# Fused packed attention and gated MLP on one core: small score and weight products gathered into fewer groups on the TensorE

## The chip, the cores and the metric

The kernel runs on one core of a Trainium2 chip. A core has a TensorE (PE) for matrix products, VectorE (DVE), ScalarE (ACT) and GpSimd (POOL) for the rest, and SyncE (SP), which here only issues DMAs. Each engine works through its own list of instructions in order. Products land in PSUM, eight banks of 512 fp32 columns on 128 partitions; all else lives in SBUF. The metric is the device time of one execution in microseconds.

## The reference

There are B = 8 batches, 8 heads, 576 tokens and 64 channels a head; `p` has 32 packing rows a head. Two attentions in a row are followed by a gated MLP over all 4608 tokens.

```python
p_packed = sm_attn(p, k, v)          # 32 rows attend to 576 tokens
out = sm_attn(q, p_packed, p_packed) # 576 tokens attend to the 32 rows
x = out.transpose(0, 2, 1, 3).reshape(B * S, H * D)
h = x @ w_in                         # 512 -> 2048
g = h * np.clip(h + 3.0, 0.0, 6.0) / 6.0
return g @ w_out                     # 2048 -> 512
```

## The kernel before

**Blocks.** One batch is a block. Since the second attention's result is a product of its weights `a` and the packed values, the kernel multiplies the packed values (`pps`) with `w_in` first; that small product is called M, and a block's first big product is M times `a`. Both are kept as a high and a low fp32r part (`m_hi`, `m_lo`, `a_hi`, `a_lo`), so each product takes three matmuls.

**The first phase** is block 0 with everything that the start needs: weights are loaded and put into parts, block 0's attention and MLP are computed, and block 1's attention is prepared. Its order is written out by hand in the text `PLAN`: each word takes one step of a chain, and within it the instructions of PE, DVE, ACT, POOL and SP are issued as the words stand. `ENGINES` says which engine does some of the copies and subtractions.

**Blocks 1 to 7** run as two chunks of tokens (256 and 320 columns). The order in each engine's list is chosen by a planner when the program is built, from dependencies, priorities and what is written as fixed. In a chunk the loop goes over 16 slices f of 128 hidden columns. `first_product` (L996) writes h = M[f] a into one of two PSUM banks (`ps_hh`), at most 320 of its 512 columns; `gate_into` makes the gate from it (ACT at L1007, then DVE at L1008); the gate's parts are split on ACT, DVE and POOL; a second product (L1036) adds to four accumulator banks. Twelve slices go as six pairs in a scheme with seven products for two slices (`pair_product`, 21 matmuls of 256 columns); its combined blocks of `w_out` are T1, T2, T3 and T4, of which some are kept in DRAM and fetched again (`fetch_t`, the `wt` steps). The last four slices are single (`single_product`, 6 matmuls of 512 columns). Second products are held back in `pend` by one or two slices.

**The next block's work** is woven into this loop by `fill`, called twice for each slice. `STEPS` gives, for each block and chain, the half-slices (0 to 63 over both chunks) at which the chain takes a step:

- `in`, `pack`: loads of the next block's k, q, v, p; the first scores `u_s1`, the exponentials, the transposes `u_ets`, the product with v `u_pvs`, and `u_ppt`, which writes `pps`.
- `ahead`: the second scores `u_s2` and the softmax on DVE and ACT that makes `a`.
- `soon`, `late`: M for the next block, a quarter (4 slices, 512 columns) at a time, with `w_in` fetched again from DRAM into one buffer (`w_in0`, L1451); three quarters in this block, the fourth early in the next.

All scores and M are products of tiles with 64 rows and 32 columns of PE, eight at a time over four pairs of heads and two halves (`each_head`, matmuls at L412). In blocks 2 to 7 they are written to a PSUM pair of their own (`att_pair`), as eight separate groups per block: two halves of 288 columns of the first scores, two of the second, and four quarters of M. In each group the PE order is fixed (`manual_schedule`).

**Room.** The next block's loads of k, q and v go through two SBUF buffers with the tag `nat`. M has four homes of a quarter each, which change roles between even and odd blocks (`m_tiles`).

Of the kernel before, what the change touches and what calls it, by code (L numbers as in the profile page):

```python
# [36 lines left out]
    },  # L37
# [7 lines left out]
    },  # L45
# [7 lines left out]
    },  # L53
# [7 lines left out]
    },  # L61
# [7 lines left out]
    },  # L69
# [7 lines left out]
    },  # L77
    7: {
        "in": "",
        "pack": "",  # L80
        "ahead": "",
        "soon": "",
        "late": "2 4 6 8",
        "wt": "10 14 42 46",
# [10 lines left out]
s0 s0 warm q1 e0 q1 c0 c0 q0 e0 v0 q0 e1 v0 v0 c1 li0 a0 a0 in s1 s1 b2 qr in a0 a0 v0 z0 c1 qr z0 z0a z0a z0a  # L95
z0a e1 v1 li2 a2 a2 a2 z0a z0a v1 z0a z0a in q2 in li1 q2 q3 q3 v1 v1 z1 m0 z0a a2 z1 a1 a1 a1 z0a z0a a1 z1b
m0 z1b z1a li3 a3 a3 z1a upper m0 m0 z1b z1b a3 z1a z1b z1a m0 lo0 z0a b0 li4 a4 a4 z1a z1a a3 z1b b0 b0 z1b
z1a z1a m1 b0 lo1 b1 m2 z1b z1b z1b z1a z1a z1a li7 a7 lp z1b b1 b1 b1 h0 warm h0 a7 a7 r0 warm r0 m1 li5 m1
h1 m1 m1 y0 b0 b0 b1 r0 lo3 b3 lo5 r0 a7 h1 b3 b3 b1 x0 x0 x0 x0 r1 r1 li6 m2 m2 h2 m2 m2 h2 r1 r1 x1 x1 x1 y0
a6 a6 a6 a5 b5 a4 b3 y1 y1 a4 r2 lk0 lk2 tk0 a6 x1 r2 h3 h3 lo4 lo6 a5 a5 a5 r2 r2 x2 tk2 m4 b3 b3 x2 x2 x2  # L100
lk3 lk1 b4 b4 b4 b4 b5 b5 li8 tp r3 y3 r3 tk3 b6 m4 m4 m4 m4 h4 h4 y2 b6 r3 r3 x3 b4 b4 b5 b5 y3 r4 y4 b6 b6
x3 tk1 r4 y4 a8 a8 a8 a8 x3 below r4 S S li9 y2 x3 b5 S S S S h5 b6 b6 r4 a9 a9 a9 li10 a10 a10 a10 h5 lq1 a10
r5 r5 lo8 tq1 S x4 S a9 r5 r5 x4 x4 x4 h6 h6 b8 b8 b8 y5 r6 r6 b8 li11 a11 a11 a11 x5 x5 x5 b8 x5 a11 h7 h7
lo7 b7 r6 r6 b7 y5 r7 y7 S m8 S lo9 b9 b9 b8 b7 lq3 lo10 r7 x6 x6 x6 x6 li12 tq3 li13 m8 lq2 m8 h8 lq0 r7 m8
m8 h8 b7 b7 r7 b7 x7 x7 x7 b10 b10 y6 y6 b10 y7 lo12 lv r8 r8 r8 r8 b9 b10 a13 a13 S S b10 tq2 h9 h9 r9 r9 x8
x8 b9 a13 b10 x7 a12 x8 a12 tq0 y8 b9 r9 x8 S S S E b12 y9 y9 E b12 h10 h10 y8 r10 y10 E E E a13 r9 b9 x9 S x9
a12 a12 r10 b12 h11 E h11 r10 r10 x10 lo11 b11 b11 b11 b11 S E lw0 lw1 V r11 r11 li14 V V x10 a14 a14 a14 T T
x9 x9 Z b12 b12 li15 a15 a15 a15 x10 x10 r11 a14 Z Z Z b11 Z y11 r11 a15 lo15 b15 b15 m12 m12 b11 b15 b15 x11
x11 m12 m12 m12 h12 h12 b12 Z lo13 b13 b13 y10 b13 y11 r12 y12 r12 r12 Z b13 b13 b13 Z x11 r12 Z x11 h13 h13
x12 x12 lo14 x12 r13 r13 h14 h14 b15 b15 r13 r13 Z Z Z y12 b14 b14 b14 r14 Z Z r14 y13 x13 x13 x12 Z h15 h15  # L110
b14 Z b14 b14 x13 x13 r14 r14 x14 x14 x14 y13 r15 r15 r15 y14 Z Z r15 x15 x15 x14 Z Z Z Z o0 o1 o0 o1 y15 Z Z
Z y14 M stage M M M M y15 x15 x15 o3 o3 o2 o2
# [21 lines left out]
def packed_attention_moe(  # L134
# [38 lines left out]
    mp = [ctx.enter_context(tc.tile_pool(name="mp", bufs=1))]  # L173
# [112 lines left out]
    def coarse(part):  # L286

        for stop in part:
            if stop is None:
                yield  # L290
# [11 lines left out]
    state, steady = {}, []  # L302

    def on(name, engine):
# [7 lines left out]
    def m_tiles(b, n):  # L312
        if ("m", b, n) not in state:
            if b % 2 == 0 and n < NCH - 1:
                n_ = NCH - 2 - n
            else:
                n_ = n
# [1225 lines left out]
```

## Time and profile before

| what | value |
|---|---|
| median of three runs | 709.0 us (707.68 to 710.12) |
| the profiled execution | 707.82 us |
| its span, first to last instruction | 705.9 us |
| DVE, ACT, POOL busy | 501.0, 429.2, 383.2 us |
| DMA traffic | 107.50 MB, 152 GB/s on average |

The span is shorter than the time of the same execution by what lies before the first and after the last instruction, 1.9 us. Busy times of different engines run beside each other. A row of the view of groups gives line, engine, operation and tiles, then the count, the busy time in us, the mean length of one in ns, and the idle time of the engine before them with what ended it. In the timeline a row gives start and length in us. A matmul's length there includes its passage through the array, so that successive ones overlap: what one costs is the distance between starts.

### The profile page before, as it was taken

To read this page: it belongs to the slowest core of one execution; us is meant where nothing else is said; L and a number is where in the kernel's file an instruction comes from. 1 tells how busy PE (TensorE), PEld (TensorE's weight loads), DVE (VectorE), ACT (ScalarE), POOL (GpSimd) and SP (SyncE) were. 2 spreads that over 40 slices of the span, in tenths; PEclk is the share of its full clock that TensorE was granted. 3 is DMA by queue.
4 is the path that set the end of the run, shared out by engine and by line. 5 is a ranking of instruction groups with operands and counts; after the bars stand their busy time and mean duration, and the time that the engine had idled before them with its cause. 6 is when DMAs were issued, how large, how long until landed. Compare 5 with 4: busy or idle time off the path is not lost.

```text
span 705.9 us, 16233 instructions
## 1 busy us (share of the span) xinstructions
PE 691.9 (98%) x5944; PEld 595.6 (84%) x5944; DVE 501.0 (71%) x1093; ACT 429.2 (61%) x1013; POOL 383.2 (54%) x615
## 2 busy tenths in 40 slices
PE   8799999999999999999999999999999999999997
PEld 6587876878878988899898998899898998889997
DVE  4898778868899669765687657876488766874443
ACT  4798876546666646565466655666366664755453
POOL 2456642744645456466464554666454546657563
PEclk9999999999999999999999999999999999999999
DMA  9979952964428665554545756383443945341030
GB/s 275 333 185 269 201 141 113 281 129 116 122 105 233 139 152 206 138 154 100 122 188 149 155 127 197 121 203 86 127 166 122 183 103 182 120 137 43 32 105 31
DMA packets 199104, 107.50 MB, mean 152 GB/s; under 512 B 173424, under 2 KB 185200, under 8 KB 195440
## 3 DMA queue, kind: packets, MB, share of 16 engines
q1 hardware_dynamic: 198480, 106.26, 55.1%
q8 instruction: 47, 0.77, 0.5%
q14 instruction: 33, 0.27, 0.1%
q10 hardware_dynamic: 544, 0.20, 0.1%
HBM read 89.65 MB, written 16.78 MB: 151 GB/s over the span
## 4 chain that ended last, share of the span: by engine, by line
PE 80%; DMA 6%; DVE 6%; ACT 3%; issue 2%; POOL 2%; SPq 1%; DVEq 0%; POOLq 0%; ACTq 0%
PE acc L1036 45%; PE ps_hh L996 23%; PE ps L412 6%; PE ps_h L669 3%; DMA raw_in<-in_moe_w_in_dram 2%; PE ps L1036 2%; DMA raw_out<-in_moe_w_out_dram 1%; DMA w_again<-w_kept 1%; PE ps L532 1%; DMA nat<-in_q_dram 1%; SPq L356 1%; DMA p_nat<-in_p_dram 1%; PE ps L502 0%; ACT t L1332 0%; DVE t L1008 0%
## 5 line engine op out<-in xcount | busy, mean ns | idle before, releaser
L996 PE MATMUL ps_hh<-a_hi,m_hi 128*128 128x320 f32 (+1 forms) x448 | 133.8, 299 | 0.3 <-DVE t L1008 0.3
L996 PE MATMUL ps_hh<-a_hi,m_lo 128*128 128x320 f32 (+1 forms) x448 | 132.9, 297 | 0.0
L996 PE MATMUL ps_hh<-a_lo,m_hi 128*128 128x320 f32 (+1 forms) x448 | 132.9, 297 | 0.0
L1008 DVE SCALAR_TENSOR_TENSOR t<-t,ps_hh 128x320 f32<-128x320 f32 (+1 forms) x148 | 66.1, 447 | 75.9 <-ACT t L1007 72.3
L1036 PE MATMUL acc<-wo_hi,g 128*128 128x512 f32 x288 | 103.4, 402 | 0.0
L1007 ACT ACTIVATE t<-ps_hh,three 128x320 f32<-128x320 f32 (+1 forms) x148 | 73.7, 501 | 47.5 <-PE ps_hh L996 40.0
L1014 POOL TENSOR_TENSOR gf<-tb,gf 128x256 fp32r<-128x256 f32 x76 | 61.6, 811 | 66.6 <-ACT gf L1013 60.0
L996 PEld LDWEIGHTS ps_hh<-a_hi,m_hi 128*128 128x128 f32 x448 | 84.7, 189 | 7.6 <-DVE t L1008 2.6
L996 PEld LDWEIGHTS ps_hh<-a_lo,m_hi 128*128 128x128 f32 x448 | 84.7, 189 | 4.3 <-issue 1.4
L996 PEld LDWEIGHTS ps_hh<-a_hi,m_lo 128*128 128x128 f32 x448 | 84.7, 189 | 2.9 <-issue 2.5
L1014 POOL TENSOR_TENSOR g<-t,g 128x256 fp32r<-128x256 f32 x72 | 54.4, 758 | 37.1 <-ACT g L1013 33.8
L1036 PE MATMUL acc<-wt,ga 128*128 128x256 f32 x456 | 74.3, 283 | 0.0
L1036 PE MATMUL acc<-wo_hi,ge 128*128 128x256 f32 x304 | 71.3, 284 | 0.0
L1036 PEld LDWEIGHTS acc<-wo_hi,g 128*128 128x128 f32 x288 | 52.7, 189 | 15.4 <-POOL bnd L1032 2.5
L1036 PEld LDWEIGHTS acc<-wt,ga 128*128 128x128 f32 x456 | 63.3, 190 | 0.7 <-issue 0.5
L1014 POOL TENSOR_TENSOR ga<-t,ga 128x256 fp32r<-128x256 f32 x76 | 61.8, 814 | 1.4 <-ACT ga L1013 1.1
L1036 PEld LDWEIGHTS acc<-wo_hi,ge 128*128 128x128 f32 x304 | 53.2, 190 | 6.1 <-ACT ga L1013 2.5
L1036 PE MATMUL acc<-wo_lo,g 128*128 128x512 f32 x144 | 56.8, 395 | 0.0
L617 DVE STREAM_TRANSPOSE tr<-nat 128x576 f32<-128x576 f32 x56 | 42.6, 766 | 17.7 <-DMA nat<-in_q_dram 9.1
L1007 ACT ACTIVATE tb<-ps_hh,three 128x256 f32<-128x256 f32 (+1 forms) x76 | 38.0, 499 | 26.9 <-PE ps_hh L996 26.1
L1032 POOL COPY bnd<-t 128x64 f32<-128x64 f32 x76 | 21.8, 286 | 58.4 <-DVE t L1008 53.0
L1278 POOL TENSOR_TENSOR tb<-tb,t 128x128 f32<-128x128 f32 x76 | 38.0, 500 | 28.3 <-DVE t L1273 22.9
(226 smaller groups left out, 1844.9 us busy)
## 6 DMA issues: line engine op xcount, KB each, us to landing
w_again<-w_kept SPq DMA_DIRECT2D x24, 1024.0 KB, 4.9
wt<-t_kept SPq DMA_DIRECT2D x24, 768.0 KB, 5.0
out_dram<-osb SPq DMA_DIRECT2D x33, 256.0 KB, 2.6
nat<-in_k_dram SPq DMA_DIRECT2D x112, 72.0 KB, 2.8
nat<-in_q_dram SPq DMA_DIRECT2D x112, 72.0 KB, 2.9
raw_in<-in_moe_w_in_dram SPq DMA_DIRECT2D x10, 512.0 KB, 6.3
raw_out<-in_moe_w_out_dram SPq DMA_DIRECT2D x10, 512.0 KB, 4.9
w_kept<-w_in_sb SPq DMA_DIRECT2D x4, 1024.0 KB, 7.6
```

The lines of the kernel that those rows point to most:

```text
L356: nc.sync.dma_start(out=t[r:r + 32], in_=src[b, 2 * a + h, :, 32 * c:32 * c + 32].rearrange("(t i) j -> i t j", i=32),)
L412: nc.tensor.matmul(pair[x][NPK * a:NPK * a + NPK, :n], rows[half, a], c, start=True, stop=True)
L532: nc.tensor.matmul(pair[x][cols, :D], l, r, start=(c == 0), stop=(c == NST - 1))
L617: nc.vector.transpose(out=t, in_=state.pop(("nat", which, b, a)))
L669: nc.tensor.matmul(h[:, hf, :HS], mm[:, g, fs], aa[:, hf * HS:(hf + 1) * HS], start=(g == 0 and i == 0), stop=(g == NG - 1 and i == 2),)
L996: state["first"] = nc.tensor.matmul(h[:, :n], mm[:, g, fs], aa[:, t0:t0 + n], start=(g == 0 and i == 0), stop=(g == NG - 1 and i == 2),)
L1007: state["relu"] = nc.scalar.activation(out=t[:, :n], in_=h, func=AF.Relu, bias=three)
L1008: state["gate"] = nc.vector.scalar_tensor_tensor(out=t[:, :n], in0=t[:, :n], scalar=6.0, in1=h, op0=ALU.min, op1=ALU.mult)
L1014: engine.tensor_sub(out=lo, in0=x, in1=hi.bitcast(F32))
L1032: nc.gpsimd.tensor_copy(out=bnd[:, f, side * REM:side * REM + REM], in_=t[:, boff:boff + REM])
L1036: nc.tensor.matmul(out, lhs[x], rhs[y], start=first and i == 0, stop=last and i == 2, skip_group_check=True)
L1278: nc.gpsimd.tensor_sub(out=s4, in0=b1, in1=s2)
```

## The change

**One stay for all scores.** In blocks 2 to 7 the 576 columns of a score product are written in one fixed group. 512 go to the PSUM pair as before; 64 go beside the first products, to columns 320 to 383 of the two `ps_hh` banks that were used last (`tops`). The copies out of PSUM follow the new split.

```diff
-    def both_halves(at_once, lhs, rhs):
-
-        if at_once:
+    def all_scores(lhs, rhs, one=None):
+
+        def tokens(cols):
+            return lambda a, half: rhs[a][half].rearrange("p t i -> p (t i)")[:, cols]
+
+        pair, few, more = att_pair(), slice(NB, S), slice(0, NB)
+        beyond = [tops[x][:, SPARE:NB - P] for x in range(2)]
+        at_once(
+            lhs,
+            (beyond, tokens(few)),
+            *([([tops[x][:, NB - P:] for x in range(2)], lambda a, half: one[half, a])] if one else []),
+            (pair, tokens(more)),
+        )
+        return (few, beyond), (more, pair)
+
+    def at_once(rows, *rounds):
+
+        with tc.manual_schedule(engines={mybir.EngineType.PE}), tc.high_priority():
+            for banks, cols in rounds:
+                for a in range(NPAIR - 1, -1, -1):
+                    for x in (1, 0):
...
```

**M in three stays and a piece.** M's 16 slices are made as 1 + 5 + 5 + 5: slice 0 with the second scores (128 columns in `ps_hh`), then slices 8 to 11 with 6, 2 to 5 with 7, and 12 to 15 with 1, each stay with 512 columns in the pair and 128 in `ps_hh`. The kept `w_in` has a new layout in DRAM, and each fetch comes as a large piece (1 MB) and one slice (256 KB), the slice in a `nat` buffer. M lives in one tile for slices 12 to 15 and one for the other twelve, with a new table of homes (`m_home`, `m_at`).

```diff
+    def u_m_wide(b, f, side):
+
+        four, one = state.pop(("w4", f)), state.pop(("w1", side))
+        yield tops
+        pair = att_pair()
+        beyond = [tops[x][:, SPARE:SPARE + P] for x in range(2)]
+        at_once(
+            pps[b % 2],
+            (beyond, lambda a, half: one[half, a]),
+            (pair, lambda a, half: four[half, :, a]),
+        )
...
+    def fetch_one(f):
+        t = state["w1", f] = ap.tile([P, NPAIR, P], F32, name="w_one", tag="nat", bufs=2)
+        nc.sync.dma_start(out=t, in_=w_kept[:, f])
...
+    def soon_wide(b):
+
+        fetch_one(0)
+        yield
+        for f, side in ((8, 6), (2, 7)):
+            fetch(f, side)
+            yield
+            yield
+            yield from coarse(u_m_wide(b, f, side))
+        fetch(12, 1)
```

**Where a stay goes.** A chain that needs `ps_hh` stops before its stay and is held; the next `beside` call with room (every odd slice of a pair, every single slice) lets it go on, with its matmuls queued behind the first product just written. The gate gets high priority.

```diff
+    def go(chain):
+
+        if not any(chain is c for c in held) and next(chain, None) is tops:
+            held.append(chain)
+
+    def beside(fill, s, room=True):
+
+        if room:
+            with tc.issue_after(state["first"].ins):
+                for chain in held:
+                    next(chain)
+            held.clear()
+        fill(s + 0.5)
...
+        tops[:] = tops[-1:] + [h]
         return h[:, :n]
...
-        state["relu"] = nc.scalar.activation(out=t[:, :n], in_=h, func=AF.Relu, bias=three)
...
+        with tc.high_priority():
+            state["relu"] = nc.scalar.activation(out=t[:, :n], in_=h, func=AF.Relu, bias=three)
...
-        with tc.manual_schedule(engines={mybir.EngineType.PE}), tc.high_priority():
+        with tc.issue_after(state["turned"].ins), tc.manual_schedule(engines={mybir.EngineType.PE}), tc.high_priority():
```

The last of these stands in `u_pvs`; `turned` is the DVE copy that ends `u_ets`.

**New step tables and another order of the first phase.** All tables of `STEPS` are new (block 7 uses block 5's), and what is left of the chains is run at slice 31 instead of 31.5. `PLAN` holds the same words in another order; `ENGINES` is unchanged. The beginning of each, and one table:

```diff
-in k0 in in p p k0 k1 k1 k2 k2 lo2 in kr b2 b2 b2 b2 kr k3 k3 in in in b2 s0 s0 s0 s0 s0 s0 s1 s1 s1 s1 s1 s1
...
+in k0 in in in p lo2 k2 k0 k1 b2 in k1 in kr p kr b2 b2 k3 s0 in s0 k3 in k2 b2 s1 s0 s0 b2 s1 s1 warm s0 s1 e0
...
-        "soon": "42 44 46 48 50 52 54 56 58 60 62 62",
-        "late": "2 4 6 8",
-        "wt": "10 14 42 46",
...
+        "soon": "31 39 39 44 47 53 53 53 54 55 55 55",
+        "late": "1 6 7 13 15 15 20",
+        "wt": "14 23 45 47",
...
```

More of the change, by code (lines that the diff above doesn't have):

```diff
@@ L99 @@
[L99 to L103, printed above, removed]
@@ L113 @@
+x14 r15 x14 r15 Z Z x14 r15 x15 Z x15 x14 Z Z Z Z o0 o1 Z M Z o0 y14 o1 y13 stage M M y15 M x15 M x15 y15 o2 o3
+o2 o3
 """
 ENGINES = {
[9 rows of a table removed]
[10 rows of a table added]
 }
@@ L310, in copy, with more_m, m_home, m_at @@
         (engine.copy if engine is nc.scalar else engine.tensor_copy)(out=dst, in_=src)
[L312 to L317, printed above, removed]
-            j = (n_ + 1) % NCH if b else 0
-            state["m", b, n] = tuple(
-                mp[j > 0].tile([P, NG, NB], F32R, name=f"m_{part}", tag=f"m_{part}{j}") for part in ("hi", "lo")
-            )
-        return state["m", b, n]
+    m_room = []
+    def more_m(pool, n):
+        m_room.append({
+            part: pool.tile([P, NG, n * NB], F32R, name=f"m_{part}", tag=f"m_{part}{len(m_room)}") for part in ("hi", "lo")
+        })
+    more_m(mp, 1)
+    def m_home(b, f):
+        if b == 0 or f >= 3 * FPC:
+            return 0, f % FPC
+        if b == 1:
+            return 1, (f + 2 * FPC) % (3 * FPC)
+        if f < 2:
+            return 1, 11 - f
+        near = (8, 9, 10, 11, 6)
+        if f in near:
+            return 1, near.index(f) + FPC * (b % 2) + b % 2
+        return 1, (2, 3, 4, 5, 7).index(f) + 5 * (1 - b % 2)
+    def m_at(part, b, f, n=1):
+        room, at = m_home(b, f)
+        return m_room[room][part][:, :, at * P:(at + n) * P]
+    def m_parts(b, f, n, banks):
+        for x, ps in enumerate(banks):
+            hi, lo = (m_at(part, b, f, n)[:, x] for part in ("hi", "lo"))
+            nc.scalar.copy(out=hi, in_=ps)
+            yield 1
+            nc.vector.tensor_sub(out=lo, in0=ps, in1=hi.bitcast(F32))
+            yield
     def u_m0(fs, bank=None, ahead=0):
@@ L342, in u_m0 @@
         yield
-        hi, lo = m_tiles(0, 0)
-        to = slice((fs[0] % FPC) * P, (fs[0] % FPC + n) * P)
-        for x, ps in enumerate(banks):
-            nc.scalar.copy(out=hi[:, x, to], in_=ps[:, :n * P])
-            yield
-            nc.vector.tensor_sub(out=lo[:, x, to], in0=ps[:, :n * P], in1=hi[:, x, to].bitcast(F32))
+        for _ in m_parts(0, fs[0], n, [ps[:, :n * P] for ps in banks]):
             yield
@@ L422, in scores, with both_halves, each_half @@
         return [[s[:, :HS] for s in pair] for pair in each_head(lhs, *(cols(hf) for hf in halves))]
-    def both_halves(at_once, lhs, rhs):
-        if at_once:
+    def all_scores(lhs, rhs, one=None):
[15 more added lines that the diff above has]
+                    for x in (1, 0):
+                        half = slice(64 * x, 64 * x + 64)
+                        nc.tensor.matmul(
+                            banks[x][NPK * a:NPK * a + NPK], rows[half, a], cols(a, half), start=True, stop=True
+                        )
+    def both_halves(joined, lhs, rhs, one=None):
+        if steady:
+            yield tops
+            yield from all_scores(lhs, rhs, one)
+            return
+        for part in each_half(joined, lhs, rhs):
+            yield part and (slice(part[0] * HS, part[0] * HS + HS), part[1])
+    def each_half(joined, lhs, rhs):
+        if joined:
             done = scores(lhs, rhs, 0, 1)
@@ L441, in u_s1 @@
         for part in both_halves(b == 1, pt, kt):
-            if part is None:
-                yield 1
+            if part is None or part is tops:
+                yield tops if part is tops else 1
                 continue
-            hf, banks = part
+            cols, banks = part
+            hf = int(cols.start > 0)
             for x, s in enumerate(banks):
-                nc.scalar.copy(out=e[x][:, hf * HS:(hf + 1) * HS], in_=s)
+                nc.scalar.copy(out=e[x][:, cols], in_=s)
                 yield 1
                 nc.vector.reduce_max(out=mx[x][:, hf:hf + 1], in_=s, axis=AX.X)
-                yield None if x else 1
+                yield None if x and not (steady and hf) else 1
         for x in range(2):
@@ L549, in u_s2 @@
         z = [ap.tile([P, T, NPK], F32, name="z", tag="e", bufs=4) for _ in range(2)]
-        for part in both_halves(not roles, pps[b % 2], qt):
-            if part is None:
-                yield 1
+        one = state.pop(("w1", 0), None)
+        for part in both_halves(not roles, pps[b % 2], qt, one):
+            if part is None or part is tops:
+                yield tops if part is tops else 1
                 continue
-            hf, banks = part
+            cols, banks = part
             for x, s in enumerate(banks):
-                nc.vector.transpose(out=z[x].rearrange("p t n -> p (t n)")[:, hf * HS:(hf + 1) * HS], in_=s)
-                yield None if x else 1
+                nc.vector.transpose(out=z[x].rearrange("p t n -> p (t n)")[:, cols], in_=s)
+                yield None if x and not (steady and cols.start) else 1
+            if one and cols.start:
+                for _ in m_parts(b, 0, 1, [tops[x][:, NB - P:] for x in range(2)]):
+                    yield 1
         for x in range(2):
@@ L588, in u_a, with u_m @@
         yield
-    def u_m(b, *ns):
-        def cols(n):
-            return lambda a, half: w_in_sb[n][half, :, a]
-        rounds = each_head(pps[b % 2], *(cols(n) for n in ns))
+    def u_m(n):
+        banks, = each_head(pps[1], lambda a, half: w_in_sb[n][half, :, a])
         yield
-        for n, banks in reversed(list(zip(ns, rounds))):
-            hi, lo = m_tiles(b, n)
-            for x, ps in enumerate(banks):
-                nc.scalar.copy(out=hi[:, x], in_=ps)
-                yield 1
-                nc.vector.tensor_sub(out=lo[:, x], in0=ps, in1=hi[:, x].bitcast(F32))
-                yield
+        yield from m_parts(1, FPC * n, FPC, banks)
+    def u_m_wide(b, f, side):
+        four, one = state.pop(("w4", f)), state.pop(("w1", side))
+        yield tops
+        pair = att_pair()
[4 more added lines that the diff above has]
+            (pair, lambda a, half: four[half, :, a]),
+        )
+        yield 1
+        for _ in m_parts(b, side, 1, beyond):
+            yield 1
+        yield
+        yield from m_parts(b, f, FPC, pair)
     def behind_gates():
@@ L1111, in moe @@
                 pend.append(gemm2)
-                fill(f + 0.5)
+                beside(fill, f)
                 second(2)
@@ L1477, in fill @@
                 for _ in range(steps["late"].count(s)):
-                    next(late, None)
+                    go(late)
                 if b == 1:
@@ L1491, in fill @@
                 for _ in range(steps["soon"].count(s)):
-                    next(soon, None)
-                if s == 31.5 and more:
-                    rest(soon)
-                    fetch_w_in(NCH - 1)
+                    go(soon)
             with tc.issue_after(state["load"].ins), behind_gates():
@@ L1498, in fill @@
                     for _ in range(steps[name].count(s)):
-                        next(chain, None)
-                if s == 31.5:
-                    rest(inputs, packed, ahead)
+                        go(chain)
+                if s == 31:
+                    rest(inputs, packed, ahead, soon)
         for c in range(2):
```

97 lines of the change are left out of this document (45 added, 52 removed), and 97 rows, old and new, of tables (ENGINES, STEPS).

## The prediction

> **What bounds the kernel now.** I read the page's busy shares first, then the busy time by stage, then the waits of the TensorE (PE) and its timeline.
>
> ```profile
> span 705.9 us, 16233 instructions
> ...
> PE 691.9 (98%) x5944; PEld 595.6 (84%) x5944; DVE 501.0 (71%) x1093; ACT 429.2 (61%) x1013; POOL 383.2 (54%) x615
> ```
>
> PE is busy for 691.9 of 705.9 us. By stage (columns: PE, PE weight load, DVE, ACT, POOL busy, then clock, DMA):
>
> ```profile
> 0.00:10.00 10.00, 8.30 (x58) 5.98 (x58) 3.02 (x7) 2.68 (x4) 1.00 (x8) 1.00 0.83 251
> 10.00:20.00 10.00, 6.77 (x161) 4.86 (x161) 6.90 (x18) 7.32 (x21) 3.79 (x3) 1.00 1.11 315
> 20.00:30.00 10.00, 8.74 (x133) 6.55 (x139) 8.06 (x23) 6.68 (x14) 5.40 (x4) 1.00 1.09 351
> 30.00:40.00 10.00, 9.12 (x62) 7.17 (x47) 8.58 (x22) 9.72 (x22) 5.45 (x4) 1.00 0.91 221
> ...
> 352.00:436.00 84.00, 84.00 (x774) 74.89 (x774) 61.50 (x137) 50.21 (x125) 46.45 (x75) 1.00 0.60 163
> ```
>
> Half of PE's 14 us of idle time lies in the first 40 us (1.70+3.23+1.26+0.88 = 7.07 us). The stretch of about one block has PE busy throughout, at full clock. After 187 us the view of waits has only two for PE:
>
> ```profile
> PE ps L412 <- DMA w_again<-w_kept: 0.6, 1, 0.6
> ...
> PE ps L532 <- DMA v_high<-in_v_dram: 0.2, 1, 0.2
> ```
>
> So in blocks 2 to 7 a microsecond that PE doesn't have to work is a microsecond of the kernel, and a wait put before PE costs its full length.
>
> **The stays, and what each costs.** A stay is a group of small 64x32-tile matmuls (line 412) that breaks into the stream of 128x128 ones. The groups by line count them:
>
> ```profile
> L412 PE MATMUL ps<-w_again,pps 64*32 64x512 f32 x384 | 26.1, 601 | 0.6 <-DMA w_again<-w_kept 0.6
> ...
> L412 PE MATMUL ps<-tr,pps 64*32 64x288 f32 x208 | 9.3, 414 | 0.0
> L412 PE MATMUL ps<-tr,p_tr 64*32 64x288 f32 x208 | 9.3, 414 | 0.0
> ```
>
> A round is 16 instructions. 384/16 = 24 stays make M for blocks 2 to 7, four a block. 208/16 = 13 rounds each for the first scores (p_tr) and the second (pps): two a block, and one each from the first phase's joined stays. The busy time doesn't give a stay's price, since it also delays its neighbours; the starts around it do. An M stay, a score stay, and the first phase's stay of two rounds (288 columns each):
>
> ```profile
> 363.53 0.28 PE L996 MATMUL ps_hh<-a_lo,m_hi 128*128 128x256 f32 x1
> 363.65 0.28 PE L996 MATMUL ps_hh<-a_hi,m_lo 128*128 128x256 f32 x1
> 363.86 1.09 PE L412 MATMUL ps<-w_again,pps 64*32 64x512 f32 x16
> 364.88 0.38 PE L1036 MATMUL acc<-wo_hi,gf 128*128 128x256 f32 x1
> 365.10 0.28 PE L1036 MATMUL acc<-wo_lo,gf 128*128 128x256 f32 x1
> ```
> ```profile
> 395.35 0.28 PE L996 MATMUL ps_hh<-a_hi,m_lo 128*128 128x256 f32 x1
> ...
> 396.20 0.39 PE L1036 MATMUL acc<-wo_hi,gf 128*128 128x256 f32 x1
> 396.43 0.28 PE L1036 MATMUL acc<-wo_lo,gf 128*128 128x256 f32 x1
> ```
> ```profile
> 53.32 0.40 PE L1036 MATMUL acc<-wo_lo,gh 128*128 128x512 f32 x1
> 53.55 0.40 PE L1036 MATMUL acc<-wo_hi,gl 128*128 128x512 f32 x1
> 53.88 0.72 PE L412 MATMUL ps_w<-tr,p_tr 64*32 64x288 f32 x16
> 54.39 0.69 PE L412 MATMUL ps<-tr,p_tr 64*32 64x288 f32 x16
> 55.01 0.50 PE L1036 MATMUL acc<-wo_hi,gh 128*128 128x512 f32 x1
> 55.35 0.39 PE L1036 MATMUL acc<-wo_lo,gh 128*128 128x512 f32 x1
> ```
>
> A 256-column matmul costs 363.65-363.53 = 0.12 us from start to start, a 512-column one 53.55-53.32 = 0.23. M stay: 365.10-363.65 = 1.45, less two at 0.12, is 1.21 us. Score stay: 396.43-395.35 = 1.08, less 0.24, is 0.84. Two rounds in one stay: 55.35-53.55 = 1.80, less 0.46, is 1.34, where two score stays cost 1.68. From 512 against 288 columns: (1.21-0.84)/224 = 1.65 ns a column, and 0.84-288x1.65 ns = 0.365 us fixed for a stay. The 576 columns of the double stay then give 1.315; it took 1.34, so a further round costs about 0.025 beyond its columns.
>
> **Merged stays, term by term.** The columns that pass through PE in a block stay the same; the entries into tile mode fall from eight to five.
> Before: 4x0.84 + 4x1.21 = 8.20 us a block.
> After, first scores (64+512 columns): 1.34. Second scores with the M piece (64+128+512): 0.365 + 704x1.65 ns + 2x0.025 = 1.58. M stays (128+512), three: 3 x (0.365 + 640x1.65 ns + 0.025) = 4.34. Sum 7.26.
> Gain 0.94 us a block; six blocks (2 to 7, the last M stay of each in the next block): **5.6 us**. Without a charge per round it is 3x0.365x6 = 6.6.
> A 64-column round isn't in the trace. Below lies its column time, 64x1.65 ns = 0.11; above, the row nearest to it, the pack product's 64-column matmuls:
>
> ```profile
> 582.56 1.30 PE ps L532 x80
> ```
>
> 16 of them take 1.30/5 = 0.26 us, with two on each column strip. I take 0.13, the round's share of the 1.34, since 64x32 tiles don't share strips so; the upper end adds 0.13x12 = 1.6 us. The page "TensorE: Matmul & The Clock Gate" of the Trainium skill ("Wait — 56ns, not 53.3ns?") says that matmul starts are never closer than about 25 ns. By it 16 would take 0.40 us and the 12 such rounds an estimated 3.2 us more; the trace disagrees, with 1.30/80 = 16 ns from start to start.
>
> **The new wait.** The 64- and 128-column rounds go to columns 320 to 511 of the two first-product banks (ps_hh). Such a stay must follow the gate's reads of both banks, and a later first product into such a bank must follow the copies out of it. That is 30 stays (5x6). One product, its gate, and the next product into the same bank (380.58; 378.04 went to the other):
>
> ```profile
> 376.99 0.29 PE L996 MATMUL ps_hh<-a_hi,m_lo 128*128 128x256 f32 x1
> 377.38 0.47 ACT L1007 ACTIVATE t<-ps_hh,three 128x256 f32<-128x256 f32 x1 [0.36 <-PE ps_hh L996]
> 377.88 0.42 DVE L1008 SCALAR_TENSOR_TENSOR t<-t,ps_hh 128x256 f32<-128x256 f32 x1
> ...
> 380.58 0.28 PE L996 MATMUL ps_hh<-a_hi,m_hi 128*128 128x256 f32 x1
> ```
>
> The gate ends at 378.30, 1.0 us after the product; then the bank is idle for 2.28 us. Two covers are needed. Before the stay PE needs 1.0 us of other work, which the pending pair product has:
>
> ```profile
> 436.07 2.49 PE acc L1036 x21
> ```
>
> After the first round, the bank has 0.85 us of the 512-column round (512x1.65 ns) plus what is left of that product. In it must go two short copies and two short subtractions, on two banks. Near rows in two blocks:
>
> ```profile
> L599 ACT CAST m_hi<-ps 128x512 fp32r<-128x512 f32 x16 | 9.3, 583 | 2.9 <-DVE m_lo L601 2.8
> L601 DVE TENSOR_TENSOR m_lo<-ps,m_hi 128x512 fp32r<-128x512 f32 x16 | 10.9, 682 | 3.5 <-ACT m_hi L599 3.4
> L1013 ACT CAST ga<-tb 128x128 fp32r<-128x128 f32 x24 | 7.2, 298 | 3.7 <-POOL tb L1278 3.2
> L1264 DVE TENSOR_TENSOR t<-t 128x128 f32<-128x128 f32 x24 | 8.9, 371 | 0.7
> ```
>
> 128 columns cost 0.30 on ACT and 0.37 on DVE: with the second bank behind, about 1.04 us, against 0.85+1.5. It fits, unless long instructions such as L601's 0.68 us stand ahead on DVE. Queued behind a late stay on PE are the pending products and the next first product, for which ACT and DVE wait in turn. Bounds: nothing, and 0.4 us a stay (12 us). I take 0.02 a stay, **0.6 us**, nearest to the row's 2.28 us of idle bank. Below nothing it can't go: the stays are added constraints on these banks.
>
> **The rest.** M's copies: 8 at 583 and 8 at 682 ns become 6 of each plus 8 short ones of each: ACT +8x0.298-2x0.583 = +1.2 us a block, DVE +8x0.371-2x0.682 = +1.6, hidden beside PE (DVE 61.5 of 84 us); uncovered they cost up to that much. High priority on the gates adds nothing, and works for the cover above. The order put around the pack product names a DVE copy, while its block holds PE instructions only; I cost it at nothing. M's single large tiles change addresses, not instructions. The two waits above, 0.6 and 0.2, may go, since three fetches of weights replace four; I take half, **-0.4 us**; both ends, -0.8 and 0.
> Each fetch now also has a 256 KB piece, which needs one of the two buffers of the q, k and v loads; these, the output stores and the fetches of T wait behind it on SP's queue. I cost that at nothing, as they are issued many microseconds ahead; see the rival.
> First phase: the same instructions on the same engines. Its chain to 23.5 us:
>
> ```profile
> 5.24 8.62 DMA raw_in<-in_moe_w_in_dram
> ...
> 15.37 8.16 DMA raw_out<-in_moe_w_out_dram
> ```
>
> These loads aren't shortened by another order of matmuls; an exchange such as k2 ahead of k1 can hold PE in program order. I take 0, bounds -1.5 and +2 us (fractions of the 7.07 us of idle PE). New step tables elsewhere move stays inside a full stream: 0.
>
> **Sum.** -5.6 + 0.6 - 0.4 = -5.4. The profiled execution took 707.8 us (span 705.9 and 1.9 around it): 702.4. The median of three runs is 709.0, 1.2 above it, which gives 703.6. I predict **703.0**, between.
>
> **Rivals.**
> *Banks that come late (ends slower).* If the gate of the current product comes after PE has spent its pending work, PE stands at the stay, for the next first product is behind it in the same banks. For: the gate needs 1.0 us at best; at single chunks only 6 matmuls at 0.23 = 1.4 us are pending. Against: 2.28 us of idle bank, 2.49 of pair product. At 0.2 us for each of 30 stays the gain is gone (709); at 0.4 it is 715. It decides from 0.27 us a stay on. The page "PSUM — Partial Sum Buffer" of the Trainium skill ("PSUM bank collisions raise a hardware error") forbids two engines in one bank and quadrant at the same time even at different columns; by it this wait can't be dropped by splitting columns. No run here shows that.
> *Loads behind the 256 KB pieces.*
>
> ```profile
> SPq L1451 <- PE ps L412: 87.2, 17, 9.8
> ```
>
> SP already stands up to 9.8 us at a fetch of weights until an M stay is over. If the shared buffers stretch that into one PE wait of 0.6 us per block, 6x0.6 = 3.6: 706.6. Against: of the present 24 fetches PE felt one.
> *Rounds pay like stays.* The change then merges nothing: 64-column rounds at the upper end and the full edge again for each extra round, 707 to 709. Against: the double stay, 1.34 and not 1.68.
> *More than the sum.* No charge per round, both waits gone, the first phase 1.5 shorter: 699 to 700.5.
>
> **Chances.** Forecast (700.5 to 705.5) 0.63; late banks 0.15 (0.08 near 709, 0.07 above 711); loads 0.10 (half of it on either side of 706.9); rounds 0.02; more 0.10. Faster by over 0.3% (about what a measurement of this kernel tells from no change; below 706.9): 0.63+0.05+0.10 = 0.78. Same: 0.08+0.05+0.02 = 0.15. Slower: 0.07. The range 699.0 to 708.0 leaves out the late banks and the tail of the rest.
>
> **What would show it.** In the profile after: line groups with 30 stays in blocks 2 to 7 instead of 48, two or three rounds back to back in each; starts around an M stay 1.45 us apart beyond neighbours; a block some 0.9 us shorter; PE still busy throughout. Wrong would be PE waits on ACT or DVE at a stay or at the first product behind it, w_one or nat among PE's releasers, or a first phase whose end moved by over 2 us.

## The result and the profile after

The changed kernel took 716.3 us (median of 4 runs, 714.18 to 718.21), the kernel before 708.8 beside it. The ratio is **1.0106, 95% interval 1.0082 to 1.0129**: about 7.5 us slower, where 703.0 was forecast and 708 was the upper end. The profiled execution took 714.18 us.

The head of the page, as it was read before:

```profile
span 712.3 us, 16908 instructions
...
PE 690.0 (97%) x6232; PEld 602.3 (85%) x6232; DVE 500.3 (70%) x1129; ACT 429.9 (60%) x1049; POOL 382.5 (54%) x615
```

PE has 1.9 us less to do than before (690.0 against 691.9) and the span is 6.4 longer, so PE stands still 22.3 us and not 14.0. The 8.3 us more are what has to be found; TensorE is still what bounds the kernel. (That only 1.9 us of busy time went, where 5.9 us of stays will turn out to be saved, suggests that some of the loss lies in what the page counts as busy.) PE's waits between 30 and 130 us (us in total, times, longest):

```profile
PE ps_h L748 <- DVE t L1414: 3.5, 1, 3.5
PE ps L355 <- POOL w_in_sb L258: 2.2, 1, 2.2
PE ps_h L748 <- DVE mx L500: 1.7, 1, 1.7
PE ps_hh L1074 <- issue: 1.5, 1, 1.5
...
```

and between 190 and 705 us:

```profile
PE ps_hh L1074 <- DVE t L1088: 2.2, 3, 1.6
PE ps_hh L461 <- DVE tb L1088: 1.0, 3, 0.5
PE ps_hh L1074 <- DVE m_lo L341: 0.3, 1, 0.3
```

Before, this was the longest entry of the first view, and the second view had only the two waits for DMAs that the prediction shows:

```profile
PE ps_h L669 <- DVE mx L449: 0.7, 1, 0.7
...
```

So most was lost before block 1, and the two DMA waits went, but waits for VectorE's gates came in. Against the kernel before, PE's first product of M and `a` starts 2.45 us later, the 14th 5.9, the first one of block 1 6.35, and the end is 6.4 later. The first one of block 1, before and after:

```profile
119.35 0.41 PE L996 MATMUL ps_hh<-a_hi,m_hi 128*128 128x320 f32 x1
```
```profile
125.70 0.38 PE L1074 MATMUL ps_hh<-a_hi,m_hi 128*128 128x320 f32 x1 [1.48 <-issue]
```

**Blocks 1 to 7 come out even: what the stays save is lost again inside them.**

The stays themselves did what they were to do. The groups at their line:

```profile
L461 PE MATMUL ps<-w_again,pps 64*32 64x512 f32 x288 | 19.2, 589 | 0.0
L461 PE MATMUL ps_hh<-w_one,pps 64*32 64x128 f32 x384 | 10.7, 279 | 0.8 <-DVE tb L1088 0.8
L461 PE MATMUL ps<-tr,pps 64*32 64x512 f32 x96 | 6.7, 594 | 0.0
L461 PE MATMUL ps<-tr,p_tr 64*32 64x512 f32 x96 | 6.4, 589 | 0.0
```

A round is 16, so 480 of the 512-column ones are 30 stays, where there were 48. Around an M stay, a stay of first scores and one of second scores with the M piece, the timeline has these starts:

```profile
374.06 0.28 PE L1116 MATMUL acc<-wo_hi,ga 128*128 128x256 f32 x1
374.27 0.45 PE L461 MATMUL ps_hh<-w_one,pps 64*32 64x128 f32 x16
374.52 1.06 PE L461 MATMUL ps<-w_again,pps 64*32 64x512 f32 x16
375.51 0.50 PE L1116 MATMUL acc<-wo_hi,ge 128*128 128x256 f32 x2
375.85 0.28 PE L1116 MATMUL acc<-wo_hi,gf 128*128 128x256 f32 x1
...
404.47 0.40 PE L1116 MATMUL acc<-wt,ga 128*128 128x256 f32 x2
...
406.15 0.28 PE L1116 MATMUL acc<-wo_hi,gf 128*128 128x256 f32 x1
...
432.64 0.28 PE L1116 MATMUL acc<-wo_lo,ge 128*128 128x256 f32 x1
...
434.48 0.28 PE L1116 MATMUL acc<-wo_lo,ge 128*128 128x256 f32 x1
```

375.85-374.06 less three matmuls at 0.12 is 1.43 us for an M stay (1.447 in the prediction), 406.15-404.47 less 0.36 is 1.32 (1.34), 434.48-432.64 less 0.24 is 1.60 (1.58). A block's stays thus cost 1.32+1.60+3x1.43 = 7.21 us, against 8.20 before: 0.99 a block, 5.9 in six.

### The profile page after: what moved, and what is told of

It reads as the page before. It is cut to its first block, busy times and chain, and to the rows that moved or that the text cites. A ratio compares the mean times of both kernels' runs of the same rounds, so it can differ in the third digit from the quotient of the medians.

```text
span 712.3 us, 16908 instructions
## 1 busy us (share of the span) xinstructions
PE 690.0 (97%) x6232; PEld 602.3 (85%) x6232; DVE 500.3 (70%) x1129; ACT 429.9 (60%) x1049; POOL 382.5 (54%) x615
## 4 chain that ended last, share of the span: by engine, by line
PE 61%; DVE 3%; DMA 2%; SPq 1%; POOL 1%; issue 1%; ACT 0%; DVEq 0%; ACTq 0%; POOLq 0%
PE acc L1116 34%; PE ps_hh L1074 19%; PE ps L461 3%; PE ps L1116 2%; PE ps_hh L461 1%; SPq L371 1%; DMA nat<-in_k_dram 1%; PE ps L583 1%; PE ps L553 1%; DMA wt<-t_kept 1%; DVE tr L697 1%; DVE t L1088 0%; POOL ga L1094 0%; DMA out_dram<-osb 0%; ACT t L1087 0%
## 5 line engine op out<-in xcount | busy, mean ns | idle before, releaser
L1088 DVE SCALAR_TENSOR_TENSOR t<-t,ps_hh 128x320 f32<-128x320 f32 (+1 forms) x148 | 66.4, 449 | 89.8 <-ACT t L1087 87.2
L1116 PE MATMUL acc<-wo_hi,g 128*128 128x512 f32 x288 | 99.5, 397 | 0.0
L1116 PE MATMUL acc<-wt,ga 128*128 128x256 f32 x456 | 79.2, 283 | 0.1
L1116 PEld LDWEIGHTS acc<-wt,ga 128*128 128x128 f32 x456 | 65.9, 190 | 1.6 <-issue 0.8
L1094 POOL TENSOR_TENSOR ga<-t,ga 128x256 fp32r<-128x256 f32 x76 | 58.0, 763 | 6.5 <-ACT ga L1093 6.0
L1112 POOL COPY bnd<-t 128x64 f32<-128x64 f32 x76 | 23.1, 304 | 63.9 <-DVE t L1088 61.5
L1116 PE MATMUL acc<-wt,gf 128*128 128x256 f32 x228 | 50.3, 285 | 0.0
```

Of the source, the lines that this page charges most:

```text
L1088: state["gate"] = nc.vector.scalar_tensor_tensor(out=t[:, :n], in0=t[:, :n], scalar=6.0, in1=h, op0=ALU.min, op1=ALU.mult)
L1094: engine.tensor_sub(out=lo, in0=x, in1=hi.bitcast(F32))
L1112: nc.gpsimd.tensor_copy(out=bnd[:, f, side * REM:side * REM + REM], in_=t[:, boff:boff + REM])
L1116: nc.tensor.matmul(out, lhs[x], rhs[y], start=first and i == 0, stop=last and i == 2, skip_group_check=True)
```

## The experiments

Two questions: what in the first phase costs 6 us, and what eats the saving in blocks 1 to 7. Ratios are to the kernel before on the same chip, with 95% intervals.

**Is it the order of the first phase?** One kernel keeps the whole change and takes back `PLAN`; the other is the kernel before with nothing but the new `PLAN`.

```diff
 PLAN = """
-in k0 in in in p lo2 k2 k0 k1 b2 in k1 in kr p kr b2 b2 k3 s0 in s0 k3 in k2 b2 s1 s0 s0 b2 s1 s1 warm s0 s1 e0
+in k0 in in p p k0 k1 k1 k2 k2 lo2 in kr b2 b2 b2 b2 kr k3 k3 in in in b2 s0 s0 s0 s0 s0 s0 s1 s1 s1 s1 s1 s1
...
```

> The changed kernel with the first phase's order (PLAN) of the kernel before; all else as changed. Theory A (the new order of the first phase costs its whole loss): block 1's first product starts as before, near 119 us instead of 125.7, and the time falls by 6.4 us from the changed kernel, to 709 to 711 us, with the stalls beside the shared banks still there. Theory B (the loss comes from the shared banks and the step tables): under 2 us of change, 714 us or more. If the merged stays bring their full 5.6 us once the order is back, it would be 703.

> The kernel before with the new order of the first phase alone; scores, M and step tables as before. Theory A: slower than before by about the 6.4 us that the first product of block 1 starts later in the changed kernel, 714 to 716 us. Theory B: within 2 us of before.

Measured: 711.2 us, ratio 1.0025 (1.0007 to 1.0043), and 714.8 us, 1.0090 (1.0060 to 1.0121). The order alone costs some 6 us of the 7.5; the rest of the change, forecast at -5.4 us, comes out at +2. Theory A thus holds in its times (711.2 lies just above its 709 to 711), but not in its place: in the trace with the old order block 1's first product still came at 122.14 us (at 119.71 once the table below is mended too), and in the trace with the new order alone at 122.26, 2.9 us later than before, while the end came 6.7 later. Less than half of what the order costs lies ahead of block 1; with the 3.5 us that follow below, these 2.9 make up the 6.35 of the changed kernel.

**The early transpose.** In the changed kernel the longest wait has this beginning (timeline: start, length, then in brackets the idle time before it and what ended it):

```profile
100.12 1.81 SPq L391 DMA_DIRECT2D p_nat<-in_p_dram  x4
...
101.72 0.40 PE L1116 MATMUL acc<-wo_hi,gl 128*128 128x512 f32 x1
...
104.61 0.31 DVE L399 STREAM_TRANSPOSE p_tr<-p_nat 128x128 f32<-128x128 f32 x1 [3.28 <-DMA p_nat<-in_p_dram]
104.85 0.72 DVE L1414 SCALAR_TENSOR_TENSOR t<-t,ps_h 128x576 f32<-128x576 f32 x1
...
105.62 0.40 PE L748 MATMUL ps_h<-a_hi,m_hi 128*128 128x288 f32 x1 [3.50 <-DVE t L1414]
```

L399 transposes block 2's p. Block 1's table `in` now begins with 0 0 0 (0 2 7 before), so its load and the transpose are asked for at block 1's very start, and the planner put the transpose among VectorE's work of the first phase. There it stands 3.28 us for a load issued at 100.12; the gate L1414 is queued behind it, and PE's next first product behind the gate. Two runs change only this table, one with the old order of the first phase and one with the new:

```diff
 STEPS[1]
-        "in": "0 0 0 3 4 14",
+        "in": "0 2 2 3 4 14",
```

> The changed kernel with the order of the first phase of the kernel before, and block 1's input table begun with 0 2 2 instead of 0 0 0. Theory (a stream transpose of block 2's p, put by the table among the vector instructions of the first phase, waits there for its load, and a gate and a first product stand behind it): with the old order alone the stretch at 102 to 110 us held 1.9 us of TensorE standstill (7.93 of 10 us busy at 100 to 110); these go, so about 709.3 us where the old order alone took 711.2, ratio to the kernel before about 1.000. Rival (the standstill comes from the first phase's last loads, whatever stands in the vector queue): stays at 711.

> The changed kernel with its own order of the first phase, and only block 1's input table begun with 0 2 2 instead of 0 0 0. Theory (the early transpose costs what its TensorE wait shows, 3.5 us at 102 us, in this order): about 712.8, ratio 1.0055. Rival (another wait for the same loads takes its place): 715 to 716.

Measured: 709.0 us, 0.9987 (0.9968 to 1.0005), and 711.8 us, 1.0045 (1.0029 to 1.0062). That one entry of a table is worth 0.38% (2.7 us) with the old order and 0.61% (4.3 us) with the new, each to some 0.25 to 0.3%; the theory held in both.

**Do the shared banks eat the saving?** This was the rival that the prediction feared most. The run with the old order and the mended table is the base; the 64- and 128-column rounds then go to the stay's own pair, where the next round overwrites them. When a stay may start is still tied to a first product, as in the change.

```diff
-        beyond = [tops[x][:, SPARE:SPARE + P] for x in range(2)]
+        beyond = [pair[x][:, :P] for x in range(2)]
```

> As the run without the early transposes, but the 64- and 128-column rounds of blocks 2 to 7 go to columns of the stay's own two banks, and not to the ends of the two first-product banks. They are overwritten there, so the scores of the last 64 tokens and the 128-column slices of M hold other values; the number of matmuls, copies and subtractions and their sizes are the same. Theory (the saving of the merged stays, 4.8 us, is given back because the first products wait for late gates and copies in the shared banks): 3 to 5 us less than the run without the early transposes, about 705. Rival (the saving is given back by the new tables, which put the stays and copies at other steps, whatever bank they use): no more than 1 us less.

Measured: 708.4 us, 0.9978 (0.9958 to 0.9999), on the same chip and in the same rounds as its base. 0.6 us less at the medians, well inside the intervals, where the theory wanted 3 to 5: the waits at the shared banks are not it. PE's waits after 30 us, of the base and then of this run:

```profile
PE ps_hh L1074 <- DVE t L1088: 2.7, 4, 1.6
PE ps_hh L461 <- DVE tb L1088: 1.8, 2, 1.2
...
```

```profile
PE ps_hh L1075 <- DVE t L1089: 1.5, 3, 0.7
...
PE acc L1117 <- POOL ga L1095: 0.8, 1, 0.8
...
PE acc L1117 <- ACT osb_j L1330: 0.7, 2, 0.3
...
```

The waits named after the banks shrink, and waits at other places (for ga, for the edge's store) come instead. So this list told where PE stood, not what would be gained.

**Do the tables?** The kernel before, its stays unmerged, with the new tables alone (and the mended figure):

```diff
 STEPS[3]
-        "in": "0 2 4 6 8",
-        "pack": "20 20 22 22 24 24 26 26 28 28 30 30 32 32 34 34",
+        "in": "1 1 17 17 18 20",
+        "pack": "21 21 21 21 21 25 25 27 28 28 28 28 28 28 28 28 30 30 30 31 31 31 31 34 34 34 34 37 43 54",
...
```

> The kernel before, its stays unmerged and its order of the first phase kept, with the new step tables alone (block 1's input table begun with 0 2 2; block 7 with the entries of block 5 that it can use). In the merged kernel with these tables the stays, their entries and exits took 5.9 us less than before and the standstill between ordinary products grew by 5.9. Theory 1 (the tables put copies and stays where VectorE is full): the same standstill without the saving, 713 to 715. Theory 2 (the standstill comes with the merged stays, which hang at fixed places behind a gate, where the single stays of before could fill a pause): the tables alone cost nothing, 708 to 709.5.

Measured: 715.3 us, 1.0079 (1.0051 to 1.0107); theory 1 held, a little above its 713 to 715 us. With the same tables, unmerged stays take 1.0079 and merged ones 0.9987: **at equal tables the merging is worth 0.92%, 6.5 us** (each ratio to some 0.2 to 0.3%). In this figure lie also the gates' high priority and the other small parts of the change, which no run takes singly. The traces say the same. For every pair of successive matmuls of the large tiles between 122 and 702 us I took the distance of their starts less the normal one (0.120 us for 256 columns, 0.148 for 320, 0.233 for 512) as standstill, and all the rest as stays with their entries and exits:

| kernel | stays, us | standstill between ordinary products, us |
|---|---|---|
| before | 68.0 | -3.0 |
| before, new tables | 68.9 | 3.6 |
| old order, table mended (merged stays) | 62.1 | 3.0 |
| the same, own banks | 61.3 | 2.5 |

(The zero is a convention: the normal distances are rounded up a little.) Merging takes 6 to 7 us out of the first column; the new tables put 6 into the second, merged or not. The waits of the kernel before with the new tables, after 110 us:

```profile
PE acc L1036 <- ACT ga L1013: 2.4, 2, 1.2
PE ps L412 <- DMA w_again<-w_kept: 1.6, 3, 1.0
PE ps_hh L996 <- DVE t L1008: 1.3, 2, 1.0
...
```

They are not the same waits as in the merged kernel. The tables were made for merged stays, so this run shows that another set of steps can cost 6 us by itself, not that each wait of the merged kernel is there without merging.

**Can the standstill be shifted away?** The largest single one of the merged kernel with the mended table:

```profile
207.97 0.42 DVE L1224 TENSOR_TENSOR wt<-wx,wt 128x256 fp32r<-128x256 f32 x1 [0.27 <-ACT wt L1223]
...
208.47 0.74 POOL L1219 TENSOR_TENSOR wx<-wo_hi,wo_lo 128x256 f32<-128x256 f32 x1 [2.80 <-DVE wt L1224]
...
209.24 0.42 DVE L1230 TENSOR_TENSOR wx<-wx 128x256 f32<-128x256 f32 x1 [0.85 <-POOL wx L1219]
...
210.04 0.41 DVE L1088 SCALAR_TENSOR_TENSOR t<-t,ps_hh 128x256 f32<-128x256 f32 x1
...
210.51 0.39 PE L1074 MATMUL ps_hh<-a_hi,m_hi 128*128 128x256 f32 x1 [1.60 <-DVE t L1088]
...
210.73 0.28 PE L1074 MATMUL ps_hh<-a_lo,m_hi 128*128 128x256 f32 x1
```

A gate (L1088) is queued on VectorE behind a step of the combine of `w_out` (L1230) that waits for POOL, and PE, with three first products in a row and its pending products used up, waits for that gate. Four runs moved entries of the tables on this base: block 2's late M stay; with it, block 1's tables of before; and two sets of shifts of half a product to one and a half.

```diff
 g1: STEPS[2]
-        "late": "0 2 2 10 19 22 30",
+        "late": "10 10 15 15",
 h4: the same, and STEPS[1] in, pack, late, t0 to t5 as in the kernel before
 m1: STEPS[1]["soon"] one half-slice earlier, STEPS[2]["ahead"] three later
 m3: the same, and STEPS[1]["pack"] one earlier
```

> The run without the early transposes, with one table more changed: block 2's late M stay (late: 0 2 2 10 19 22 30) goes to the steps of the kernel before (10 10 15 15), five products into the block and no longer at its start, where the combine of the second weights still fills VectorE. Theory (the saving of the stays is given back because the new tables put stays and copies where VectorE is full, and a gate then comes late): the wait of 1.6 us at 208 us and its restarts go, 1.5 to 2 us less than 709.0, about 707.2. Rival (each merged stay brings its stall along, wherever it stands): same stall some 13 us later, 709.

> As the run with the late stay of block 2 moved, and block 1's tables for the inputs, the pack product, the late M stays and the six combines are those of the kernel before too; the merged stays, the shared banks and the tables of blocks 3 to 7 stay the new ones. Theory (tables): standstill between ordinary matmuls after 120 us falls from 5.9 us over the kernel before to 1.5 to 2.5 us, so about 705 us, faster than both kernels. Rival (the stalls belong to the merged stays and the copies they bring): 708 to 709.

> As the run without the early transposes, with two tables shifted: block 1's fetch and M stays of block 2 (soon) half a product earlier, block 2's joined second scores (ahead) one and a half products later. There three first products no longer stand in a row behind the stay at the block's start (207 us) and at the joined scores (262 us); the first of them moves to about 200 us. Theory 1 (the standstill hangs on where each stay lets pending products run out, so it can be shifted away): the waits of 1.8 and 0.6 us go, a smaller one comes at 200; about 707, ratio 0.996 to 0.997. Theory 2 (VectorE is behind anyway between 190 and 245 us, and another product waits there instead): 708.5 to 709.5.

> As the run before it, and block 1's table for the first scores and the pack product half a product earlier, so that the three first products at 140 us have a stay between them. Theory 1: the 0.65 us there go too, 706 to 706.5, ratio 0.995 to 0.996. Theory 2: no better than the run without the early transposes, 708.5 to 709.5.

Measured: 1.0004 (0.9986 to 1.0022); 1.0093 (1.0069 to 1.0116); 1.0217 (1.0185 to 1.0250); 1.0255 (1.0221 to 1.0289). In all four the first theory missed, on the slow side, and in the last three the rival's time was missed too. In the first, the wait at 208 us stayed (1.87 us between two starts at 207.94, 1.75 more than normal) although the stay had gone, so the stay doesn't make it; and 1.7 us came at 234 us. In the second, with block 1's old combine steps, it shrank to 0.37 us, which fits the combine as its cause, but 3.05 us came at 237 us. In the last two the shift also lets block 2's slice 6 of M be copied to its place ahead of block 1's slice 8, which is read there in the second chunk, so that this product takes other values. How much of their 15 to 18 us is waiting for that copy was not separated (13.7 us of the third run's trace also ran at half clock, at most 6.8 us of it), so these two can't tell the theories apart. The first two runs speak for theory 2 in part: with a stay moved away, another product waits somewhere else. None of the four found tables that keep the saving.

**Which part of the order?** The new `PLAN` is the old one's 611 words in other places, and at words 171, 217 and 376 both have used the same words. So parts can be taken alone, on the kernel before.

```diff
 PLAN (words)
-old 1..611
+f1: new 1..171, old 172..611
+f2: old 1..217, new 218..376, old 377..611
+g3: old 1..376, new 377..611
+k1: new 1..376, old 377..611
```

> The kernel before, with only the first 171 of the 611 words of the first phase's order taken from the new one (up to and just past the first of the first products). Theory (the new order loses time at two places, in the loading stretch before the first product, where it came 2.45 us later, and at the sixth product): 1.5 to 2.5 us slower than before, about 711. Rival (the loss before the first product is hidden, since the loads set the end of that stretch, or is a stretch of half clock that comes and goes): 709.

> The kernel before, with only words 217 to 376 of the first phase's order taken from the new one (from the loads of the second half to the seventh product; h5 h5 stands there ahead of three of the S steps that copy block 1's first scores out of their bank). Theory: the sixth product waits 2.3 us for the maximum of those scores, against 0.7 before; about 2 to 2.5 us slower, 711. Rival (this wait only takes the place of a later one): 709.

> The kernel before, with only the last 235 words of the first phase's order taken from the new one. The whole new order alone cost 5.7 us at the medians (714.8 against 709.1); its first 171 words alone cost 0.0, words 217 to 376 alone 0.7. Theory (the losses add up): the rest lies here, some 4 to 5 us, 713 to 714, most of it at 181 to 189 us, where a store of the output stands in SP's queue behind loads of block 2's k and q, and TensorE stands 2 us. Rival (the losses need each other: the early parts shift loads so that the later ones collide): 709 to 710.5.

> The kernel before, with the first 376 words of the first phase's order taken from the new one. Words 1 to 171 alone cost nothing, 217 to 376 alone 0.05%, 377 to 611 alone 0.17%, all together 0.9%. Theory 1 (the two early parts need each other: the first puts the fetches of weights back, the second has the sixth product wait for them): 712 to 714. Theory 2 (the early parts push the loads of block 2 into the last part's store, so all are needed): 709 to 710.

Measured: 0.9986 (0.9967 to 1.0005), 1.0005 (0.9987 to 1.0022), 1.0017 (0.9996 to 1.0037), 1.0036 (1.0013 to 1.0058), against 1.0090 for all. The first three theories fell: none of these three parts costs alone what its waits seemed to show. Alone they sum to 0.1%; the whole order costs about 0.8%, 6 us, more. The third run came out at its rival's time, the fourth (712.7 us) within theory 1's. Whether the parts need each other isn't shown by this: words 172 to 217 stand in the fourth run and in the whole order, but were never taken alone, so the 0.4% by which the fourth exceeds the first two may be theirs; and the fourth and the third add up to 0.53%, which intervals of 0.2 to 0.3% don't tell from 0.90. One place where parts act together is the full new order at 180 to 190 us. ACT's waits there:

```profile
ACT osb L986 <- DMA out_dram<-osb: 3.2, 1, 3.2
```

A store of the result of block 1's first chunk is late, ACT waits for its buffer, and PE stands 2.0 us for ACT. With the last part alone PE stood 1.6 us at this place, with the first part alone 1.4, with the first 376 words 0.5. Only the 2.0 us were followed by half clock (last section), 3.4 us of it, which is some 1.7 us. The wait and the half clock together make some 3.7 us, all by which this trace falls further behind after block 1's start. That the late store hangs on loads ahead of it on SP's queue was argued, not tried; in the trace its copy is done at 177.1 us, and SP issues it at 181.38, right behind six loads of block 2's k that it began at 172.66.

## Why the prediction was wrong

- **What bounds the kernel: right.** PE is busy 97% of the span, and it stands still 8.3 us more.
- **Merged stays, -5.6 us: right.** 1.43, 1.32 and 1.60 us a stay against 1.447, 1.34 and 1.58, 5.9 us in six blocks; 6.5 by the ratios at equal tables. The charge per round and the 0.13 for a 64-column round held.
- **The new wait on the shared banks, +0.6: not contradicted.** Taking the sharing away gave 0.6 us, not told apart from nothing, so that the figures agree is luck. The view of waits (3.5 us at `ps_hh` after 190 us) would have misled here. The rival of late banks named 709 to 715 us and gave 0.07 to more than 711; the time came near, for other reasons.
- **Old waits, -0.4:** w_again and v_high are both gone from the list after 190 us, which is the end of -0.8 and not the half.
- **"New step tables elsewhere move stays inside a full stream: 0": this step failed.** It measured +0.79%, 5.6 us, alone. PE's stream was full because each gate came in time; the tables set when VectorE, ACT and POOL do the next block's work between the gates, and PE keeps only 1.4 to 2.5 us of pending products. The prediction asked what the moved stays cost PE, not what stood in VectorE's queue ahead of each gate at the new places. VectorE (third pair of columns) had little room there, as the kernel before shows by stage:

```profile
190.00:200.00 10.00, 10.00 (x78) 8.17 (x78) 9.82 (x22) 7.07 (x17) 6.98 (x9) 1.00 0.13 52
200.00:210.00 10.00, 10.00 (x58) 8.73 (x57) 8.75 (x19) 5.88 (x16) 5.31 (x7) 1.00 0.49 184
210.00:220.00 10.00, 10.00 (x94) 8.03 (x94) 9.90 (x25) 6.81 (x17) 3.78 (x7) 1.00 0.64 230
```

  It is busy 87 to 99% of the time around the change from block 1 to block 2, which the mean of 61.5 in 84 us that the prediction used (73%) hides. VectorE is not the whole of it: with the new tables alone PE's longest waits were for ACT's `ga` (2.4 us) and a fetch of weights (1.6).
- **"First phase: the same instructions on the same engines ... I take 0, bounds -1.5 and +2 us": this step failed too.** The order alone measured +0.90%, 6.4 us; in its trace 2.9 us of it, already more than the bound, lie ahead of block 1, and the rest where no term of the prediction looked, at a store in block 1. "The same instructions" was even untrue: block 1's `in` moved a DMA-fed transpose into the first phase's VectorE queue, another 2.7 to 4.3 us. The words 0 0 0 stood in the diff; the question of what is queued behind a step moved earlier was not put to them. Two of the prediction's own signs of being wrong were the ones that came: PE waiting for VectorE at a first product, and a first phase whose end moved by over 2 us.
- **Loads behind the 256 KB pieces, a rival of 706.6**: nothing of it is seen. No wait of PE for w_one or nat is in the list after 190 us. **Rounds that pay like stays**: the three stays above exclude it.
- **High priority of the gates and the order after `turned`, costed at nothing**, were not run by themselves.

Added up in ratios: order +0.90%, tables +0.79, early transpose +0.38 (old order), merging -0.92, sum +1.15%; measured +1.06 (0.82 to 1.29). The forecast had only the last of these terms, and took the others for nothing, or for nothing within narrow bounds. The sum tests less than it seems: the transpose and the merging are themselves quotients of these runs, so only the order is checked, 0.90% alone against 0.81% inside the change (1.0106 to 1.0025). And that these agree is partly luck, since the 2.0 us wait of the order alone at 185 us is not in the changed kernel's list.

What stays open: which words of the order cost the 2.9 us ahead of block 1, whether its parts cost more together than alone, which entries of the tables make the standstill, and whether some tables keep the 6 us of the merging.

## What to carry to other kernels

A saving on the bounding engine is only kept if the engines that feed it still deliver in time, so a change that comes with a new schedule has two prices; try the new schedule on the old code, and the new code on the old schedule, before adding them up. When a step is moved earlier, look first for the instruction in it that waits for a DMA, and then for what its engine has queued behind it. Don't take a wait's length in the profile for the gain from removing it: of the places tried here, only the DMA-fed transpose gave back what its wait showed.

## What was not expected of the hardware

After some standstills TensorE ran at half its clock. In the run with block 1's old tables (start us, us):

```profile
234.41 0.28 PE L1116 MATMUL acc<-wo_lo,ga 128*128 128x256 f32 x1
237.74 0.58 PE L1074 MATMUL ps_hh<-a_hi,m_hi 128*128 128x256 f32 x1 [3.05 <-DVE t L1088]
238.11 0.41 PE L1074 MATMUL ps_hh<-a_lo,m_hi 128*128 128x256 f32 x1
238.33 0.41 PE L1074 MATMUL ps_hh<-a_hi,m_lo 128*128 128x256 f32 x1
```

Its view by stage (columns as before; the granted clock stands ahead of the DMA share):

```profile
233.20:236.60 3.40, 1.48 (x13) 1.28 (x11) 0.00 (x1) 0.53 (x2) 1.16 (x2) 0.99 0.96 281
236.60:243.40 6.80, 5.67 (x26) 5.67 (x27) 4.99 (x12) 3.07 (x9) 3.01 (x5) 0.50 0.80 140
```

After 3.05 us of standstill the matmuls start 0.21 us apart and not 0.12, for 6.8 us, which costs another 2.4 us or so (an estimate: 5.67 us of busy time, less 0.12/0.21 of it). With the new order alone a standstill of 2.0 us was enough, for 3.4 us of half clock:

```profile
182.00:185.40 3.40, 1.39 (x12) 1.19 (x11) 0.29 (x1) 1.03 (x4) 0.61 (x3) 1.00 0.80 212
185.40:188.80 3.40, 3.40 (x28) 2.26 (x27) 2.32 (x7) 2.02 (x6) 1.82 (x4) 0.50 0.26 90
```

But the 3.5 us at 102 us in the changed kernel had no such sequel:

```profile
100.50:103.90 3.40, 1.62 (x8) 1.01 (x6) 0.83 (x3) 0.74 (x1) 1.29 (x1) 1.00 0.82 205
103.90:107.30 3.40, 1.68 (x12) 1.68 (x13) 2.67 (x5) 1.70 (x3) 0.48 (x1) 1.00 0.85 136
106.00:110.00 4.00, 4.00 (x26) 3.62 (x25) 3.95 (x8) 3.77 (x8) 1.48 (x2) 1.00 0.58 93
```

So the length of a standstill alone does not decide it; its place does. Half clock came in stretches of 3.41 us or twice that, and where a trace has two of them, their starts lie whole multiples of 3.413 us apart: 30.72 us (9) in the changed kernel with the mended table, 215.04 (63) in the run with block 1's old tables, 88.75 (26) in the last of the shifted ones. So the clock goes by windows that run on by themselves, and the first rows above are cut close to such windows (those of the changed kernel by counting on from its only stretch of half clock before the end, at 11.77 us). In the window ahead of the half clock PE stood still 2.0 us (3.40-1.39) and 1.9; the changed kernel's 3.5 us fell into two windows, 1.8 and 1.7 us. Between 40 and 700 us of all traces the clock fell six times, after windows with 1.73 to 2.95 us of standstill; the longest standstills in a window without a fall are the changed kernel's, 1.67 to 1.81. In these runs the bound thus lies near half a window.

The page "TensorE: Matmul & The Clock Gate" of the Trainium skill ("What's actually happening") says that the clock is judged in windows of some 3.4 us that run on by themselves, and falls to half after an idle one. The lengths 3.4 and 6.8 us and the whole multiples agree with such windows; that a whole window must be idle doesn't agree with the 2.0 us.

The clock is also much of the spread between executions of one kernel: on one chip the kernel before took 705.2 to 707.2 us three times at a mean granted clock of 1.000, and 711.5 and 712.1 at 0.995 and 0.994. It is not the loss of the change: at 0.997 the changed kernel took 714.2 and 714.7 us, the kernel before, on another of the chips, 707.8 to 710.5 in eight executions.

Each restart after a wait also cost 0.07 to 0.11 us more than the wait itself: behind the wait shown at 210.51 us the next matmul started 0.22 us later and not 0.12.
